# Attention and FFN in one kernel: the kernel plans the order of all engines itself

## The chip, the cores and the metric

The kernel runs on one core of one Trainium2 chip. The metric is the device time of one execution in microseconds (us), the median of 3 runs. Five instruction streams of the core matter here: TensorE (PE, with its weight loads PEld), VectorE (DVE), ScalarE (ACT), GpSimd (POOL), and SyncE (SP), which issues DMAs. Each stream runs its instructions in the order in which they were issued, so a waiting instruction holds up all that stand behind it on its engine.

## The reference, cut to what matters

Attention with 4 sink keys and a sliding window of 128 keys over 4 batches, 8 heads, 768 positions, head width 64; its output, heads side by side, is the 3072 x 512 input of an FFN with 2048 inner columns. All is float32.

```python
scores = scale * np.matmul(q, k.transpose(0, 1, 3, 2))
keep = is_sink | in_window            # in_window: 0 <= rel < window
scores = np.where(keep, scores, -1000000000.0)
scores = scores - np.max(scores, axis=-1, keepdims=True)
a = np.exp(scores)
a = a / (np.sum(a, axis=-1, keepdims=True) + 1e-09)
x = np.matmul(a, v)                   # then (B*S, H*D)
h = x @ w_in
g = np.where(pos, h, np.where(neg, 0.0, (h + beta) ** 2 / (4.0 * beta)))
return g @ w_out
```

The weights w_in and w_out arrive as 8-byte words (float64, read as pairs of int32), which the kernel turns into float32 by integer operations ("decoding").

## The kernel before

The 3072 rows are cut into 8 chunks of 384 rows (3 tiles of 128), first the first halves of the 4 batches, then the second halves. For each chunk attention is computed for 8 heads (a unit is one head of one chunk), its output is collected in `xn`, split into a high and a low part `x` (L617), and goes through the FFN.

- **FFN.** For each of 16 blocks j of 128 inner columns, `stage1` (L582) makes 12 matmuls of 384 columns into `h_ps` (high by high, high by low, low by high), then `g` by two ACTIVATEs on ACT (L595, L596) and one instruction on DVE (L597), then `gh` on ACT (L598) and `gl` by a subtraction (L599: on POOL for the first chunk, on DVE for the other seven). `stage2` (L602) makes 9 matmuls of 512 columns into three `o_ps`. It stands two j behind stage 1 (`LAG`), and the last two j of a chunk stand among the next chunk's first.
- **Attention.** The first 16 units (chunks 0 and 1) go through a path by pairs of heads in plain float32: `pair_scores` (L441 on PE, L452 on DVE, L457 on ACT), `early_transp` (L474, L476 on PE, copies on ACT), `pair_r` (L505), `pair_av` (L493, L496). The other 48 units ("native") split q, k, the probabilities and v into high and low parts, like the FFN (L254 to L405).
- **Decoding.** 16 blocks of 1 MB, by turns of w_in and w_out; each serves two j. A block takes four DVE instructions over 128 x 1024 elements (L170, L176, L179, L183) and one copy on ACT (L180). Nothing else than chunk 0's FFN waits for them, and all later chunks use the decoded weights again. Blocks 0 to 3 are loaded on SP's queue, the others on ACT's.
- **Order.** Chunk 0's attention (pairs 0 to 3, with blocks 0 to 3 decoded beside it and pair 4's scores) comes first, by a hand-written sequence (`first_pairs`, `queue`). Then the FFN of chunk c is mixed with the attention of chunk c+1 by `spread`: PE's order is that of the program, steps of both in proportion to their weights, and the decoding of blocks 4 to 15 is spread over chunk 0's FFN. On DVE, ACT, POOL and SP the framework's scheduler orders what is not tied down. The last chunk's FFN has no attention beside it.

Of the kernel before, what the change touches and what calls it, by code (L numbers as in the profile page):

```python
# [41 lines left out]
WLEAD = 0.9  # L42
# [7 lines left out]
def attn_ffn(ctx, tc, qk, qkp, vx, vs, par, w_in, w_out, out):  # L50
# [5 lines left out]
    moe3 = ctx.enter_context(tc.tile_pool(name="moe3", bufs=3))  # L56
    ps_a = ctx.enter_context(tc.tile_pool(name="ps_a", bufs=3, space=bass.MemoryType.PSUM))
# [98 lines left out]
    raw = {}  # L156
# [30 lines left out]
    def decode(t, w, words, pin=False):
        for f in decode_parts(t, w, words, pin):
            f()

    top = {}
    loaded = []

    def weights(n):

        def src(k):
            return (w_in, w_out)[k % 2][k // 2 * 2:k // 2 * 2 + 2].bitcast(I32).rearrange("j p c -> p j c")

        def fetch():
            for k in range(n, min(n + min(AHEAD if n > 2 else 1, NP // 2 - n // 2 - 1) + 1, NP)):  # L200
                if k not in raw:
                    raw[k] = wpool.tile([P, 2, 2 * DM], I32, name="w")

                    with tc.issue_after(loaded[-1]) if k < SYNC else nullcontext():
                        (nc.sync if k < SYNC else nc.scalar).dma_start(raw[k], src(k))

        def parts(on):
            j, i = n // 2 * 2, n % 2
            words = raw[n].rearrange("p j (c two) -> p j c two", two=2)
            if i:  # L210
                t = wpool.tile([P, 2, 2, DM], F32R, name="w")
                w_o[j:j + 2] = t[:, 0], t[:, 1]
            else:
                t = wi2[n // 2]
            return decode_parts(t, dec.tile([P, 2, DM], I32, name=f"bits{n % 2}"), words, pin=not on, on=on)

        def f():
            fetch()
            for g in parts(False):
                g()  # L220

        if n < WFIRST:
            return fetch, lambda: parts(True)
        return f


    again = {}
# [23 lines left out]
    fast.enter_context(tc.manual_schedule(engines={mybir.EngineType.PE}))  # L251
    st = {}

    def load(u):  # L254
        b, h, t0 = u
        T = CT * P
        W = (P if t0 else -NSINK) + CT * KB
        q_l = att.tile([P, T], F32R, name="q_l")
        q_h = att.tile([P, T], F32R, name="q_h")
        k_r = att1.tile([P, P + CT * KB], F32, name="k_r")[:, :W]  # L260
        k_s = att.tile([P, P + CT * KB], F32R, name="k_s")[:, :W]
        nc.sync.dma_start(k_r, qk[b, h, t0 // CT, :, T:T + W])
        q_r = att1.tile([P, T], F32, name="r")
        nc.sync.dma_start(q_r, qk[b, h, t0 // CT, :, :T])
        nc.scalar.copy(k_s, k_r)  # L265
        eng = nc.gpsimd if units.index(u) in KL_POOL else nc.vector
        eng.tensor_tensor(k_s[D:P], k_r[D:P], k_s[D:P].bitcast(F32), op=ALU.subtract)  # L267
        nc.scalar.copy(q_h, q_r)  # L268
        nc.gpsimd.tensor_tensor(q_l, q_r, q_h.bitcast(F32), op=ALU.subtract)  # L269
        st["qk", u] = ((q_h, q_l), k_s)  # L270

    def scores(u, i):
        b, h, t0 = u
        qs, k_s = st["qk", u]
        if i == 0:
            st["p", u] = [att.tile([P, CT, 260], F32, name="p"), att.tile([P, 2 * CT], F32, name="stat")]
# [4 lines left out]
        ps = ps_a.tile([P, 512], F32, name="ps_a")  # L281
        for j, q in enumerate(qs):
            nc.tensor.matmul(ps[:, lo:260], lhsT=q[:, i * P:(i + 1) * P], rhs=k_s[:, c0:c0 + 260 - lo],  # L283
                             start=(j == 0), stop=(j == len(qs) - 1))
        peak_i = peak[:, units.index(u), i:i + 1]
        m = (m0, m1, m2)[min(t, 2)]
        nc.vector.tensor_tensor_reduce(  # L287
            out=p[:, i, lo:260], in0=ps[:, lo:260], in1=m, scale=-0.125, scalar=3.0e38,
            op0=ALU.add, op1=ALU.min, accum_out=peak_i)
# [532 lines left out]
```

## Time and profile before

| what | value |
|---|---|
| time, median of 3 runs (lowest, highest) | 705.93 us (703.86, 706.32) |
| the profiled execution's own time | 705.98 us |
| its span, first to last instruction | 704.3 us |
| busy: PE, PEld | 681.5 us (97%), 604.6 us (86%) |
| busy: DVE, ACT, POOL | 510.3 us (72%), 489.5 us (70%), 278.8 us (40%) |
| DMA moved, mean rate | 73.98 MB, 105 GB/s |

Read it so: a busy PE is not a PE at its best rate, since an instruction that waits for data inside a run of matmuls, or runs at the lower clock, counts as busy as well. Two instructions of one engine overlap by some 0.05 to 0.1 us, so that a sum of durations is larger than the busy time of a stretch, which counts each moment once.

### The profile page before, as it was taken

How to read it: one execution, taken by the hardware profiler on the slowest of the kernel's cores; microseconds unless marked ns; L12 is line 12 of the kernel's file. 1: busy time of each engine (PE TensorE's matmuls, PEld its weight loads, DVE VectorE, ACT ScalarE, POOL GpSimd, SP SyncE). 2: the span in 40 equal slices, each digit the busy share in tenths (PEclk: the TensorE clock that was granted, in tenths of full speed). 3: DMA queues.
4: the chain of work that ended last, by engine and by line, in shares of the span. 5: the costliest groups of instructions: out<-in, count | busy, mean ns of one | idle time of the engine just before them, and what ended most of it. 6: DMA issues, size and time to landing. Idle time of an engine off the chain costs nothing.

```text
span 704.3 us, 12263 instructions
## 1 busy us (share of the span) xinstructions
PE 681.5 (97%) x3889; PEld 604.6 (86%) x3889; DVE 510.3 (72%) x1405; ACT 489.5 (70%) x1241; POOL 278.8 (40%) x470
## 2 busy tenths in 40 slices
PE   5899998999999999999999999999999999999996
PEld 3567877899999999989889999899899999989995
DVE  7888998887776877688777878878787877642221
ACT  4886667687778868777787877777776876554332
POOL 3003344744443445355554455635544444300000
PEclk9899999999999999999999999999999999999999
DMA  7864533132244344254333443434322310001001
GB/s 232 291 216 156 190 99 135 49 107 60 63 148 124 102 127 129 68 174 128 92 113 105 147 130 124 126 118 133 122 59 62 102 50 22 3 1 45 1 1 49
DMA packets 45441, 73.98 MB, mean 105 GB/s; under 512 B 10744, under 2 KB 30008, under 8 KB 45368
## 3 DMA queue, kind: packets, MB, share of 16 engines
q1 hardware_dynamic: 42104, 60.53, 28.2%
q10 hardware_dynamic: 3264, 12.58, 4.8%
q8 instruction: 33, 0.54, 0.3%
q14 instruction: 40, 0.33, 0.1%
HBM read 66.80 MB, written 6.29 MB: 104 GB/s over the span
## 4 chain that ended last, share of the span: by engine, by line
PE 79%; DVE 9%; DMA 3%; ACT 3%; POOL 3%; issue 2%; SPq 0%; ACTq 0%; POOLq 0%; DVEq 0%
PE h_ps L588 33%; PE o_ps L607 32%; PE ps_a L283 4%; PE ps_a L390 4%; PE ps_a L344 2%; DVE bits L176 2%; DVE bits L179 1%; DMA w<-w_in 1%; POOL q_l L269 1%; PE ps_a L474 1%; DVE w L183 1%; DVE bits L170 1%; PE ps_a L493 1%; DVE p L304 1%; DVE g L597 1%
## 5 line engine op out<-in xcount | busy, mean ns | idle before, releaser
L588 PE MATMUL h_ps<-x,wi 128*128 128x384 f32 x1536 | 310.2, 340 | 0.0
L588 PEld LDWEIGHTS h_ps<-x,wi 128*128 128x128 f32 x1536 | 262.2, 188 | 8.7 <-issue 1.5
L607 PE MATMUL o_ps<-w,gh 128*128 128x512 f32 x768 | 244.0, 398 | 0.0
L607 PE MATMUL o_ps<-w,gl 128*128 128x512 f32 x384 | 151.1, 393 | 0.4 <-POOL gl L599 0.4
L607 PEld LDWEIGHTS o_ps<-w,gh 128*128 128x128 f32 x768 | 134.3, 188 | 16.9 <-issue 1.7
L597 DVE SCALAR_TENSOR_TENSOR g<-g,h_ps 128x384 f32<-128x384 f32 x128 | 70.3, 549 | 61.7 <-ACT g L596 60.6
L595 ACT ACTIVATE g<-h_ps,half 128x384 f32<-128x384 f32 x128 | 73.9, 578 | 52.7 <-PE h_ps L588 52.0
L269 POOL TENSOR_TENSOR q_l<-r,q_h 128x384 fp32r<-128x384 f32 x48 | 51.1, 1064 | 122.7 <-ACT q_h L268 116.1
L598 ACT CAST gh<-g 128x384 fp32r<-128x384 f32 x128 | 65.5, 512 | 46.1 <-DVE g L597 44.9
L290 ACT ACTIVATE p<-p,peak 128x260 f32<-128x260 f32 (+1 forms) x144 | 71.5, 496 | 23.0 <-DVE peak L287 22.4
L607 PEld LDWEIGHTS o_ps<-w,gl 128*128 128x128 f32 x384 | 72.0, 188 | 17.8 <-POOL gl L599 0.7
L599 DVE TENSOR_TENSOR gl<-g,gh 128x384 fp32r<-128x384 f32 x112 | 67.3, 601 | 23.5 <-ACT gh L598 22.6
L267 DVE TENSOR_TENSOR k_s<-k_r,k_s 64x524 fp32r<-64x524 f32 (+1 forms) x44 | 49.1, 1115 | 34.4 <-ACT k_s L265 34.3
L596 ACT ACTIVATE g<-g 128x384 f32<-128x384 f32 x128 | 67.0, 524 | 2.0
L287 DVE CUSTOM_DVE_ANT_0 p<-ps_a,m 128x260 f32<-128x260 f32 (+1 forms) x144 | 57.0, 407 | 14.7 <-PE ps_a L283 13.8
L358 POOL TENSOR_SCALAR_AFFINE_SELECT pt<-pt 128x384 fp32r<-128x384 f32 (+1 forms) x96 | 51.3, 535 | 22.6 <-DVE pt L349 19.5
L304 DVE CUSTOM_DVE_ANT_0 p<-p,stat 128x128 f32<-128x128 f32 x128 | 57.0, 489 | 0.2
L356 POOL TENSOR_SCALAR_AFFINE_SELECT pt<-pt 128x384 fp32r<-128x384 f32 (+1 forms) x96 | 49.9, 521 | 8.8 <-ACT pt L348 4.9
L599 POOL TENSOR_TENSOR gl<-g,gh 128x384 fp32r<-128x384 f32 x16 | 23.4, 1461 | 67.7 <-ACT gh L598 64.2
L390 PEld LDWEIGHTS ps_a<-pt,v_s 128*128 128x128 f32 x304 | 42.4, 190 | 1.8
L390 PE MATMUL ps_a<-pt,v_s 128*128 128x256 f32 (+1 forms) x304 | 41.9, 275 | 0.0
L283 PE MATMUL ps_a<-k_s,q_h 128*128 128x260 f32 (+1 forms) x144 | 40.7, 283 | 1.2 <-DVE sk L352 0.9
(151 smaller groups left out, 933.1 us busy)
## 6 DMA issues: line engine op xcount, KB each, us to landing
r<-qk SPq DMA_DIRECT2D x48, 192.0 KB
k_r<-qk SPq DMA_DIRECT2D x32, 262.0 KB
again<-w_in SPq DMA_DIRECT2D x16, 512.0 KB
again<-w_out SPq DMA_DIRECT2D x16, 512.0 KB
w<-w_in ACTq DMA_DIRECT2D x6, 1024.0 KB
w<-w_out ACTq DMA_DIRECT2D x6, 1024.0 KB
out<-o SPq DMA_DIRECT2D x23, 256.0 KB
r<-vx SPq DMA_DIRECT2D x32, 128.0 KB
```

Source lines behind the costliest of these rows:

```text
L269: nc.gpsimd.tensor_tensor(q_l, q_r, q_h.bitcast(F32), op=ALU.subtract)
L283: nc.tensor.matmul(ps[:, lo:260], lhsT=q[:, i * P:(i + 1) * P], rhs=k_s[:, c0:c0 + 260 - lo], start=(j == 0), stop=(j == len(qs) - 1))
L290: nc.scalar.activation(p[:, i, lo:260], p[:, i, lo:260], AF.Exp, bias=peak_i, scale=-1.0, accum_out=stat[:, i:i + 1])
L304: nc.vector.tensor_tensor_reduce(out=own, in0=own, in1=p[:, i, 0:P], scale=r, scalar=0.0, op0=ALU.add, op1=ALU.add, accum_out=stat[:, i:i ...
L390: nc.tensor.matmul(z, lhsT=w, rhs=y, start=(n == 0), stop=(n == len(mms) - 1))
L588: nc.tensor.matmul(h_ps[:, :T], lhsT=w_i[j][:, w, ct * P:(ct + 1) * P], rhs=x[:, y, ct], start=(ct == 0 and n == 0), stop=(ct == NCT - 1 a ...
L595: nc.scalar.activation(g, h_ps[:, :T], AF.Relu, bias=half, scale=0.5)
L596: nc.scalar.activation(g, g, AF.Square)
L597: nc.vector.scalar_tensor_tensor(g, g, 1.0, h_ps[:, :T], op0=ALU.min, op1=ALU.max)
L598: nc.scalar.copy(gh, g)
L599: (nc.gpsimd if row0 == GL_POOL else nc.vector).tensor_tensor(gl, g, gh.bitcast(F32), op=ALU.subtract)
L607: nc.tensor.matmul(o_ps[tt], lhsT=gg[:, tt * P:(tt + 1) * P], rhs=w_o[j][:, w], start=(j == 0 and n == 0), stop=(j == NJ - 1 and n == 2))
```

## The change

The program no longer issues an instruction where the code stands. Each helper records an `op`: its engine, a length in ns, the call that issues it, and what it reads and writes (`Slot`s of a `Ring` stand for tiles that share buffers). `Plan.due` goes through PE's work in the order of the program and gives every op the latest time at which it is still of use; `Plan.order` then goes through all engines with those lengths, takes on each the ready op that is due first, and on PE the next one of two lanes, A (attention) and B (FFN), by their shares done. All instructions are then issued in that order, and no scheduler moves them on any engine.

With it come smaller edits. Decoding has other instructions: two that write single bytes into a tile `ends` (L361, L363), one that joins them with the shifted word in place (L365), the copy on ACT (L367), and the subtraction (L368): four on DVE, as before. All weight blocks are loaded on SP's queue. `gl` is computed on DVE for chunk 0 too. The values of a pair come by one DMA in place of four, and sink values from the tile `vq`, which needs no memset. Pair 4's scores are no longer in the first stage. For 2 of the native units a small addition moves from POOL to DVE (L459).

```diff
+    def due(self):
+        t = 0
+        for o in self.ops:
+            o.due = t + SOON
+            if o.eng == PE:
+                o.due = t
+                t += o.ns
+            for b in o.before:
+                b.after.append(o)
+        for o in reversed(self.ops):
+            for a in o.after:
+                o.due = min(o.due, a.due - o.ns - (2500 if o.eng == SP else DELAY[o.eng]))
...
+        def turn(t):
+            a, b = head("A"), head("B")
+            a_in, b_in = a is not None and not a.left and a.ready <= t, b is not None and not b.left and b.ready <= t
+            if a_in and b is not None and b_in:
+                if a.group[1] != b.group[1]:
+                    return a if a.group[1] < b.group[1] else b
+                ka, kb = ("A", a.group[1]), ("B", b.group[1])
+                return a if done[ka] * LEAD * total[kb] <= done[kb] * total[ka] else b
+            return a if a_in else b if b_in else None
...
-            first = nc.vector.tensor_scalar(w, x, 3, 0x3FFFFFFF, op0=ALU.logical_shift_left, op1=ALU.bitwise_and)
...
-            queue(nc.vector.scalar_tensor_tensor(w, x, -0x40000000, w, op0=ALU.bitwise_and, op1=ALU.bitwise_or), on)
...
-            queue(nc.vector.scalar_tensor_tensor(w, low, 29, w, op0=ALU.logical_shift_right, op1=ALU.bitwise_or), on)
-            queue(nc.scalar.copy(high, w.bitcast(F32)), on)
...
-            queue(nc.vector.tensor_tensor(rest, w.bitcast(F32), high.bitcast(F32), op=ALU.subtract), on)
...
+        op(SP, 420, lambda: nc.sync.dma_start(raw(), src()), r=[("w", past)] if past >= 0 else [], w=[r],
+           size=1 << 20)
+        op(DVE, 680, lambda: nc.vector.tensor_scalar(e()[..., 0], b()[..., 0, 3], 5, 0x07, op0=ALU.logical_shift_right,
+                                                     op1=ALU.bitwise_and), r=[r, "dec"], w=["ends"])
+        op(DVE, 680, lambda: nc.vector.tensor_scalar(e()[..., 3], b()[..., 1, 3], 0x80, 0xC0, op0=ALU.bitwise_and,
+                                                     op1=ALU.bitwise_xor), r=[r, "dec"], w=["ends"])
+        op(DVE, 1180, lambda: nc.vector.scalar_tensor_tensor(w(), words()[..., 1], 3, ends, op0=ALU.logical_shift_left,
+                                                             op1=ALU.bitwise_xor), r=["ends", "dec"], w=[wk, r])
+        op(ACT, 980, lambda: nc.scalar.copy(to()[:, :, 0], w().bitcast(F32)), r=[wk, "dec"], w=[(t, 0)])
+        op(DVE, 1180, lambda: nc.vector.tensor_tensor(to()[:, :, 1], w().bitcast(F32), to()[:, :, 0].bitcast(F32),
+                                                      op=ALU.subtract), r=[wk, (t, 0), "dec"], w=[(t, 1), t])
...
-        (nc.gpsimd if row0 == GL_POOL else nc.vector).tensor_tensor(gl, g, gh.bitcast(F32), op=ALU.subtract)
...
+        op(DVE, 500, lambda: nc.vector.tensor_tensor(gl(), g(), gh().bitcast(F32), op=ALU.subtract), r=[g, gh], w=[gl])
```

Three places show how the order moves. On PE, the end of chunk 0's attention and the first matmuls of its FFN (`h_ps<-x,wi`), before:

```order
L505 MATMUL ps_a<-ident,stat 64x128 x6
L493 MATMUL ps_a<-pt,vq_178 64x128 x2
L493 MATMUL ps_a<-pt,vq_178 64x256 x4
L493 MATMUL ps_a<-spn_179,vq_178 64x128
L493 MATMUL ps_a<-spn_180,vq_178 64x128
L441 MATMUL o_ps<-k_s,q_h 128x128 x2
L441 MATMUL o_ps<-k_s,q_h 128x260
L441 MATMUL h_ps<-k_s,q_h 128x260 x2
L441 MATMUL ps_a<-k_s,q_h 128x260
L474 MATMUL ps_a<-ident,p 128x128 x3
L588 MATMUL h_ps<-x,wi_155 128x384 x3
```

and now:

```order
L690 MATMUL ps_a<-ident,pt 128x128 x5
L692 MATMUL ps_a<-ident,pt 4x128
L690 MATMUL ps_a<-ident,pt 128x128 x5
L692 MATMUL ps_a<-ident,pt 4x128
L733 MATMUL ps_a<-ident,stat 64x128 x6
L811 MATMUL h_ps<-x,wi_155 128x384 x3
L713 MATMUL ps_a<-pt,vq_176 64x128 x2
L713 MATMUL ps_a<-pt,vq_176 64x256 x4
L713 MATMUL ps_a<-v_s,vq_176 64x128 x2
L648 MATMUL ps_a<-k_s,q_h 128x128 x2
L811 MATMUL h_ps<-x,wi_155 128x384 x3
```

The FFN's first matmuls move ahead of pair 3's product with the values and of all of pair 4, which stood in front of them. On DVE, the same place, before (`bits` is a block being decoded, `wi` a finished one, `xn` a pair's output):

```order
L183 TENSOR_TENSOR wi_156<-bits_389,wi_156 128x2x512
L464 TENSOR_SCALAR stat<-stat 128x2x3
L465 RECIPROCAL stat<-stat 128x2x3
L170 TENSOR_SCALAR bits_475<-w 128x1024
L496 TENSOR_TENSOR xn<-ps_a,xn 128x384
L176 SCALAR_TENSOR_TENSOR bits_475<-w,bits_475 128x1024
L619 TENSOR_TENSOR x<-xn,x 128x384
L179 SCALAR_TENSOR_TENSOR bits_475<-w,bits_475 128x1024
L496 TENSOR_TENSOR xn<-ps_a,xn 128x384
L452 ISA p,peak<-o_ps,m_109 128x128
```

and now:

```order
L363 TENSOR_SCALAR ends<-w 128x1024
L365 SCALAR_TENSOR_TENSOR w<-w,ends 128x1024
L361 TENSOR_SCALAR ends<-w 128x1024
L720 TENSOR_TENSOR xn<-ps_a,xn 128x384
L678 TENSOR_SCALAR stat<-stat 128x2x3
L680 RECIPROCAL stat<-stat 128x2x3
L368 TENSOR_TENSOR wi_155<-w,wi_155 128x2x512
L852 TENSOR_TENSOR x<-xn,x 128x384
L363 TENSOR_SCALAR ends<-w 128x1024
L365 SCALAR_TENSOR_TENSOR w<-w,ends 128x1024
L852 TENSOR_TENSOR x<-xn,x 128x384
```

Before, three blocks are finished here and the fourth is under way; now the first is just being finished and the second and third are three quarters done, and the fourth has not been begun. On POOL, chunk 0's FFN before (`gl` is the FFN's low part, `k_s` and `q_l` belong to native units):

```order
L599 TENSOR_TENSOR gl<-g,gh 128x384 x7
L267 TENSOR_TENSOR k_s<-k_r,k_s 64x392
L269 TENSOR_TENSOR q_l<-r,q_h 128x384
L599 TENSOR_TENSOR gl<-g,gh 128x384 x3
L267 TENSOR_TENSOR k_s<-k_r,k_s 64x392
L269 TENSOR_TENSOR q_l<-r,q_h 128x384
```

and on POOL now:

```order
L895 MEMSET ends 128x1024
L292 TENSOR_TENSOR tsel<-tsel_125 120x3
L426 TENSOR_TENSOR q_l<-r,q_h 128x384
L423 TENSOR_TENSOR k_s<-k_r,k_s 64x392
L426 TENSOR_TENSOR q_l<-r,q_h 128x384
L423 TENSOR_TENSOR k_s<-k_r,k_s 64x392
```

The 16 subtractions of `gl` are gone from POOL and stand among DVE's instructions. Up to the last instruction of decoding, DVE's queue holds the same 64 decoding instructions, 8 pairs and 15 `g` as before, 14 `gl` more, and the normalisation of one native unit instead of two.

## Rows read from the trace of the kernel before

**Rows 1.** The page, busy us of each engine, share of the span, instructions.
```profile
PE 681.5 (97%) x3889; PEld 604.6 (86%) x3889; DVE 510.3 (72%) x1405; ACT 489.5 (70%) x1241; POOL 278.8 (40%) x470
```
**Rows 2.** Windows of stages: length, busy (instructions) by engine, clock, DMA.
```profile
core 0: us, PE busy (x) PEld busy (x) DVE busy (x) ACT busy (x) POOL busy (x), PEclk, DMA share, GB/s
0.00:4.90 4.90, 0.05 (x2) 0.08 (x2) 3.56 (x19) 1.28 (x1) 1.37 (x11) 1.00 0.50 137
4.90:42.70 37.80, 30.16 (x223) 20.75 (x224) 31.62 (x101) 28.34 (x93) 5.13 (x25) 0.91 0.82 270
42.70:133.20 90.50, 88.34 (x531) 71.31 (x530) 80.79 (x140) 60.16 (x152) 37.72 (x30) 1.00 0.42 143
...
294.00:378.30 84.30, 83.71 (x474) 75.60 (x473) 65.28 (x192) 64.61 (x164) 43.25 (x72) 1.00 0.40 120
...
625.90:697.80 71.90, 71.82 (x360) 64.31 (x358) 21.08 (x41) 30.48 (x60) 0.00 (x0) 1.00 0.03 12
```
**Rows 3.** The chain that ended last: start, length, what.
```profile
4.95 7.92 DMA w<-w_in
...
359.68 3.23 DMA r<-vx
...
427.56 2.25 DMA r<-qk
...
687.40 2.08 PE o_ps L607 x9
689.48 2.08 PE h_ps L588 x12
```
**Rows 4.** Timeline of PE, first stage: start, length, what, idle before.
```profile
22.70 0.64 PE L441 MATMUL o_ps<-k_s,q_h 64*128 64x260 f32 x1
...
37.34 0.87 PE L505 MATMUL ps_a<-ident,stat 128*64 128x128 f32 x12
...
39.72 0.71 PE L441 MATMUL o_ps<-k_s,q_h 64*128 64x128 f32 x5
...
40.26 0.38 PE L441 MATMUL o_ps<-k_s,q_h 64*128 64x260 f32 x1
...
42.72 0.77 PE L588 MATMUL h_ps<-x,wi 128*128 128x384 f32 x3
```
**Rows 5.** Timeline of DVE, decoding and the next chunk's first split.
```profile
20.69 1.21 DVE L176 SCALAR_TENSOR_TENSOR bits<-w,bits 128x1024 int32<-128x1024 int32 x1
...
35.71 0.65 DVE L170 TENSOR_SCALAR bits<-w 128x1024 int32<-128x1024 int32 x1
...
89.09 1.93 DVE L179 SCALAR_TENSOR_TENSOR bits<-w,bits 128x1024 int32<-128x1024 int32 x1
...
131.99 1.23 DVE L183 TENSOR_TENSOR w<-bits,w 128x1024 fp32r<-128x1024 f32 x1 [0.65 <-ACT w L180]
133.53 2.31 DVE L619 TENSOR_TENSOR x<-xn,x 128x384 fp32r<-128x384 f32 x3 [0.32 <-ACT x L618]
```
**Rows 6.** Timeline of POOL beside the 1.93 us instruction.
```profile
88.54 1.39 POOL L599 TENSOR_TENSOR gl<-g,gh 128x384 fp32r<-128x384 f32 x1 [3.47 <-PE ps_a L474]
```
**Rows 7.** Groups: operation, shape, count, busy us, mean ns, idle before.
```profile
L599 DVE TENSOR_TENSOR gl<-g,gh 128x384 fp32r<-128x384 f32 x112 | 67.3, 601 | 23.5 <-ACT gh L598 22.6
...
L269 POOL TENSOR_TENSOR q_l<-r,q_h 128x384 fp32r<-128x384 f32 x48 | 51.1, 1064 | 122.7 <-ACT q_h L268 116.1
...
L179 DVE SCALAR_TENSOR_TENSOR bits<-w,bits 128x1024 int32<-128x1024 int32 x16 | 22.2, 1389 | 0.2
L176 DVE SCALAR_TENSOR_TENSOR bits<-w,bits 128x1024 int32<-128x1024 int32 x16 | 21.8, 1365 | 0.3
L170 DVE TENSOR_SCALAR bits<-w 128x1024 int32<-128x1024 int32 x16 | 11.4, 711 | 2.9 <-DMA w<-w_in 2.9
L183 DVE TENSOR_TENSOR wi<-bits,wi 128x1024 fp32r<-128x1024 f32 x8 | 10.6, 1326 | 4.4 <-ACT wi L180 4.4
L183 DVE TENSOR_TENSOR w<-bits,w 128x1024 fp32r<-128x1024 f32 x8 | 9.8, 1223 | 2.4 <-ACT w L180 2.4
```

More of the change, by code (lines that the diff above doesn't have):

```diff
@@ L1 @@
[L1 removed]
+import heapq
+from contextlib import ExitStack
 import concourse.bass as bass
@@ L187, in decode @@
[L187 to L210, printed above, removed]
+        nc.vector.tensor_scalar(w, x, 3, 0x3FFFFFFF, op0=ALU.logical_shift_left, op1=ALU.bitwise_and)
@@ L211, in parts @@
                 t = wpool.tile([P, 2, 2, DM], F32R, name="w")
                 w_o[j:j + 2] = t[:, 0], t[:, 1]
[L213 to L227, printed above, removed]
+                at["t"] = t
@@ L306, in scores @@
[L306 to L309 removed]
+        first = n < NATIVE + 2
+        op(DVE if first else POOL, 100 if first else 250, lambda: (nc.vector if first else nc.gpsimd).tensor_scalar(
+            stat()[:, CT:2 * CT], stat()[:, 0:CT], 1.0e-9, None, op0=ALU.add), r=[(stat, k) for k in range(CT)],
+           w=[(stat, "r")])
@@ L558, in attn_ffn @@
+        for f in steps:
+            f()
+        pair_load(n)
     chunks = [(b, t) for t in (0, CT) for b in range(B)]
@@ new lines, in mm, with at @@
+        def mm():
+            for n, (gg, w) in enumerate(((gh, 0), (gh, 1), (gl, 0))):
+                nc.tensor.matmul(ps(), lhsT=gg()[:, tt * P:(tt + 1) * P], rhs=w_o[j][:, w],
+                                 start=(j == 0 and n == 0), stop=(j == NJ - 1 and n == 2))
+        op(PE, 693, mm, r=[("w", j // 2 * 2 + 1), gh, gl], w=[ps])
+        if j == NJ - 1:
+            end = (row0, tt) == (last, CT - 1)
+            o = ("out",) if end else out_ring.new()
+            def at():
+                return xn.rearrange("p c t -> p (c t)")[:, :DM] if end else o()
+            op(ACT, 500, lambda: nc.scalar.copy(at(), ps()), r=[ps] + [("xn", c, a) for c in range(NCT) for a in range(2)]
+               if end else [ps], w=[o])
+            op(SP, 420, lambda: nc.sync.dma_start(out[row0 + tt * P:row0 + (tt + 1) * P, :], at()), r=[o], size=1 << 18)
@@ L624, in moe_steps @@
         o_ps, hs = [], {}
-        steps = [(0.0, lambda ct=ct: split(x, ct)) for ct in range(NCT)]
+        steps = [("B", 0.0, lambda ct=ct: split(x, ct)) for ct in range(NCT)]
         second = tail[:]
@@ L658, in attn_ffn, with run @@
-    pt0 = [att.tile([P, 2, CT, 2, P], F32R, name="pt").bitcast(F32).rearrange("p a i c q -> p (a i c q)")
-           for _ in range(2)]
-    wsteps = [weights(n) for n in range(NP)]
-    n0 = 0
+    ends = dec.tile([P, 2, DM], I32, name="ends")
+    spare = dec.tile([P, 2, 2 * DM], I32, name="spare")
+    with tc.issue_after(behind):
+        nc.gpsimd.memset(ends, 0)
+    p0 = [p_ring.new() for _ in range(2)]
+    pt0 = [pt_ring.new() for _ in range(2)]
+    def run(steps, c):
+        for lane, w, f in steps:
+            plan.group = lane, c, w
+            f()
@@ L697, in attn_ffn @@
-    other = const.tile([1, 1], I32, name="other")
-    nc.vector.tensor_scalar(flag[0:1, 2:3], flag[0:1, 1:2], -1.0, 1.0, op0=ALU.mult, op1=ALU.add)
-    nc.vector.tensor_copy(other, flag[0:1, 2:3])
-    for _, f in prev + tail:
-        f()
+        b, t0 = chunks[c]
+        ffn = moe_steps(b * S + t0 * P, tail)
+        n1 = min(H * (c + 2), len(units)) + 2
+        attn = [step for n in range(n0, n1) for step in attn_steps(n)] if n0 < n1 else []
+        n0 = n1
+        if c == 0:
+            attn = [step for m in range(4, 9) for step in pair_steps(m)] + attn
+            ffn = spread([("B", 1.0, lambda n=n: block(n)) for n in range(4, NP)], ffn, LEAD)
@@ new lines, in result @@
+    def result():
+        nc.vector.tensor_reduce(flag[0:1, 1:2], ps()[0:1, :P], axis=mybir.AxisListType.X, op=ALU.min)
+        nc.vector.tensor_scalar(flag[0:1, 2:3], flag[0:1, 1:2], -1.0, 1.0, op0=ALU.mult, op1=ALU.add)
+        nc.vector.tensor_copy(other, flag[0:1, 2:3])
+    op(DVE, 4000, checks, w=["flag", "both"] + [("peak", n, i) for n in range(len(units)) for i in range(CT)])
+    ps = bank_a.new()
+    op(PE, 110, lambda: nc.tensor.transpose(ps()[0:1, :P], flag[:, 0:1], ident), r=["flag"], w=[ps])
@@ L703, in attn_ffn @@
+    op(DVE, 700, result, r=[ps], w=["flag"])
+    plan.issue()
+    region.close()
     fast.close()
```

778 lines of the change are left out of this document (472 added, 306 removed).

## The prediction

> **What bounds the kernel now.** I read the page's busy times first: PE is busy 97% of the span, DVE 72%, ACT 70%, POOL 40% [rows 1]. So PE bounds the kernel, and a new order can gain only where PE waits or runs below its best rate. Next, what PE's best rate is: at the end of the chain of waits, where the last chunk's FFN stands alone, 12 matmuls of stage 1 take 2.08 us (the chain groups them by turns with stage 2's 9, which take 2.08 us too) [rows 3]. A step j of the FFN is then 4.16 us, a chunk 16 x 4.16 = 66.6 us, and the 8 chunks 533 us.
>
> The windows then say where PE falls short [rows 2]. The last chunk alone: 71.9 us, which is 17.3 steps of 4.16 (its own 16 and the rest of the chunk before): at its best rate. A middle chunk takes 84.3 us with 83.7 of them busy, 17.7 us over the FFN's 66.6 us, in which the 8 native units' matmuls stand: nothing in this row looks like waiting. The first 133.2 us are another matter. The FFN's first matmul starts at 42.72 us [rows 4], and chunk 1 gets its first low part of x at 133.5 us [rows 5]. The work of PE to that point is 62.4 us of FFN (16 steps without the 4.16 us of the last two steps' stage 2, which come later), 8 pairs, and some 4 us of the first native units (an estimate: a middle chunk's 17.7 us are 2.2 us a unit, for less than two). A pair at full clock takes 5 us: from pair 3's L505 at 37.34 to the next pair's scores at 39.72 are 2.4 us, its transposes and scores about as much [rows 4]. That is 62.4 + 40 + 4 = 106 us against 133.2, so some 27 us are lost there: 4.9 before the first matmul, a few to the lower clock (the first stage's clock is 0.91 on the mean, and a matmul of 260 columns shows 0.64 us at 22.7 us, where 0.38 us stands at 40.3 us [rows 2, 4]), and the rest to waiting.
>
> What does PE wait for there? For DVE. DVE is busy 3.56 + 31.62 + 80.79 = 116.0 of these 133.2 us, 87%, more than anywhere later (77% in the middle chunk) [rows 2]. The 16 blocks of decoding are 11.4 + 21.8 + 22.2 + 10.6 + 9.8 = 75.8 us of it by durations [rows 7], and the last ends at 133.2 us, just before chunk 1's split [rows 5]. PE shows 88.34 of 90.5 us busy in the middle window of it [rows 2], since its instructions overlap; the sum above is the better measure.
>
> **The change, part by part.** The question is when DVE can finish decoding, and whether PE, ACT or DMA takes its place.
>
> *Decoding, on DVE.* Four instructions go, four come, so overlap cancels. The quiet prices are 0.65 us for the one-source instruction (L170) and 1.21 to 1.23 us for those with two sources [rows 5]. Their means are higher, 0.71 and 1.22 to 1.39 us [rows 7], because some take up to 1.93 us while POOL works at a subtraction [rows 5, 6]. The new block is two one-source instructions and two with two sources. Single bytes in and out do not occur on DVE in this trace, so their price is bounded: 0.65 us (the one-source row of as many elements) to 1.22 us (the two-source row) each, and above that only if bytes are handled worse than words. I take 0.65 us, the row of the same operation. With it a block is 2 x 0.65 + 2 x 1.22 = 3.74 us, 16 are 60 us; I add 2 us for the POOL work that remains: 75.8 - 62 = 14 us saved (between 16 saved and, at 1.22 us a byte instruction, 4 lost).
> [...]
>
> *gl on DVE.* 14 of the 16 stand before the last block: 14 x (0.60 - 0.08 of overlap) = 7.3 us added [rows 7]. It also takes away the 1.39 us subtractions on POOL that slow DVE [rows 6], which is in the sum above.
>
> *The rest of DVE's queue to that point.* One native unit's normalisation stands behind it now: -1.2 us; the two memsets of the value tiles are gone: -1 us; both are estimates from DVE's mean of 0.45 us an instruction (116.0 us for 260). Sum: 116.0 - 14 + 7.3 - 2.2 = 107 us of work (105 to 125 by the bounds of the byte instructions).
>
> *DVE's idle time* to that point is 133.2 - 116.0 = 17.2 us: 1.3, 6.2 and 9.7 us in the three windows [rows 2]. The first two stay by my reckoning. ACT carries 28.3 us in the 37.8 us of the first stage, and loses there about one cast and one pair's six exponentials, some 4 us of the 28: with 24 us of work after the first scores, ACT holds the FFN's start to no earlier than 30 us, ten us before now, and DVE waits for it in between. The third window is what an order by due time can fill: I halve it. DVE then ends decoding at 107 + 1.3 + 6.2 + 5 = 119.5 us (112 if nearly all idle time goes, 124 if all stays).
>
> *PE to the same point* needs its 106 us, 4.9 us of start and some 3 us at the lower clock: 114 us at the least, so PE does not forbid 119.5 us but leaves little below it.
>
> *Loads.* Block 0's load goes behind pair 2's two on SP's queue; those wait for buffers that pair 0's scores free. Now it is issued at 4.95 us and takes 7.92 us to land [rows 3], with DMA at 270 GB/s in that stage [rows 2]: bandwidth sets most of that, so I count 0 to 3 us later, covered by pair 1's and 2's scores, which DVE now has ahead of the first decoding; without that cover it costs 3 us. The twelve blocks that leave ACT's queue for SP's are paced by decoding and cost nothing while DMA stands at 42% [rows 2].
>
> *Later chunks.* PE's order of A and B steps there is almost the same as before, and PE runs there without visible waits, so I count 0 (between 4 us won and what the second rival costs). The end of the last chunk is unchanged.
>
> **Sum.** Chunk 1 starts at 119.5 instead of 133 us: -13.5 us. The profiled execution has 705.98 us with a span of 704.3, and stands at the median of 705.93: 705.98 - 13.5 = 692.5, I say 692 us.
>
> **The rivals.**
> 1. *The gain stays small*: DVE keeps all its idle time because PE, DVE and ACT hand over in turn (matmul, two ACTIVATEs, L597, cast, gl) and gl now queues behind instructions of 1.2 us each. The 9.7 us idle in the FFN's window speak for it; that gl no longer waits for 1.39 us of POOL against it. DVE ends at 124 to 130 us: 696 to 703 us, 700 in the middle.
> 2. *SP's one queue and the one buffer `r` become the bound of the later chunks.* `r` holds by turns a unit's q and its v: 2.25 us of load, 1.06 us of POOL's q_l, 3.23 us of load [rows 3, 7], and two casts on ACT and one subtraction on POOL that cost at most as much as q_l each: 6.5 to 9.7 of the 10.5 us a unit has (84.3 / 8). All engines now run in one planned order, and a load that stands behind an output DMA or a weight check on SP holds up PE, which has its next unit's scores in a fixed place. Against it: the same buffer and queue serve now, without a wait in the middle chunk's row. It decides at 13.5 / 48 = 0.3 us a native unit; with 0.5 us it is +24 - 13.5 = +10.5: 716 us, slower.
> 3. *Bytes cost DVE as much as two sources do, or more*: at 1.22 us, 32 x 0.57 = 18 us more: DVE ends at 137.5 us, 4.5 us behind now: 710 us, slower. It turns slower from 0.65 + 13.5 / 32 = 1.07 us an instruction.
> 4. *Writing every other word is slow*: L365 at the slowest two-source row, 1.93 us [rows 5], in 15 blocks: 15 x 0.71 = 10.7 us, DVE ends at 130 us: 703 us. [...]
> 5. *The plan does more than that*: PE's floor of 114 us is reached and the later chunks win up to 4 us: 682 to 687 us.
>
> **How the numbers follow.** The forecast (687 to 697 us about 692) has 0.55, rival 1 0.12, rival 2 0.07, rival 3 0.06, rival 4 0.06, rival 5 0.12, and 0.02 is left for a gain and a loss that cancel. What a measurement of this kernel can tell from no change is about 0.5%, 3.5 us: 702.4 to 709.5 us. Faster than that: the forecast, rival 5, nearly all of rival 1 and half of rival 4, 0.81. The same: the edge of rival 1, half of rivals 3 and 4 and what cancels, 0.08. Slower: rival 2, half of rival 3 and the rest, 0.11. The range that holds 8 in 10 goes from rival 5's 682 to 709 us, where rival 3 begins; the forecast's own is 687 to 697.
>
> **What would show each step.** The first FFN matmul at 30 to 35 us instead of 42.7. The byte instructions at 0.65 to 0.75 us, L365 and L368 at 1.2, none near 2 us. The last decoding's end at 115 to 124 us and chunk 1's first split there too; from then on middle chunks of 84.3 us as now, and the last at 71.9. I am wrong if the byte instructions show over 1 us, if the middle chunks are longer than 85 us with PE waiting for loads of `r`, or if the last decoding ends early and chunk 1 still starts at 130 us.

## The result, and the profile after

| | before | after |
|---|---|---|
| time, median (lowest to highest), 4 runs each on the same chip | 705.59 us (703.86 to 706.32) | 693.20 us (692.49 to 694.62) |
| ratio after / before, 95% interval | | 0.9831 (0.9806 to 0.9855) |
| profiled execution, its span | 705.98 us, 704.3 us | 692.49 us, 690.4 us |

The kernel is faster by 12.4 us, 1.7%. The busy times of the whole span hardly show it (compare [rows 1]); PE has the same 3889 matmuls:

```profile
PE 674.4 (98%) x3889; PEld 603.1 (87%) x3889; DVE 509.6 (74%) x1421; ACT 487.2 (71%) x1241; POOL 240.5 (35%) x421
```

The windows of the kernel after, cut at its own stages (start, attention before the FFN, chunk 0's FFN up to the last decoding, a middle chunk, the last chunk; columns as in [rows 2]):

```profile
0.00:4.60 4.60, 0.00 (x0) 0.01 (x1) 2.23 (x14) 1.28 (x1) 1.38 (x11) 1.00 0.47 127
4.60:28.40 23.80, 21.72 (x192) 16.07 (x192) 20.11 (x80) 20.31 (x76) 4.86 (x23) 1.00 0.82 264
28.40:119.80 91.40, 89.73 (x552) 71.79 (x551) 85.43 (x170) 66.70 (x163) 9.74 (x8) 1.00 0.52 181
282.20:365.40 83.20, 83.20 (x476) 76.54 (x475) 66.69 (x192) 63.95 (x164) 39.12 (x64) 1.00 0.41 122
610.90:683.30 72.40, 72.24 (x362) 64.78 (x360) 21.01 (x39) 31.21 (x61) 0.00 (x0) 1.00 0.03 12
```

Against [rows 2]: the first stage is 23.8 us instead of 37.8, with PE busy 91% of it instead of 80% and at a printed clock of 1.00 instead of 0.91 (the last section says where that column is not to be trusted). The stage of chunk 0's FFN is as long as it was (91.4 and 90.5 us), with more of pair 3 and all of pair 4 in it. A middle chunk is 1.1 us shorter than the 84.3 us of before, the last one is the same within 0.5 us. DVE works 2.23 + 20.11 + 85.43 = 107.8 us to the end of decoding, 116.0 before.

PE's timeline where the FFN begins (start, length, instructions), and DVE's where decoding ends and chunk 1 begins (L852 is the split of `xn` into `x`), to set against [rows 4, 5]:

```profile
27.61 0.87 PE L733 MATMUL ps_a<-ident,stat 128*64 128x128 f32 x12
28.41 0.80 PE L811 MATMUL h_ps<-x,wi 128*128 128x384 f32 x3
```

```profile
118.56 1.22 DVE L368 TENSOR_TENSOR w<-ends,w 128x1024 fp32r<-128x1024 f32 x1
...
121.42 1.42 DVE L852 TENSOR_TENSOR x<-xn,x 128x384 fp32r<-128x384 f32 x2
```

The FFN's first matmul is at 28.41 us (42.72 before), the last decoding ends at 119.8 us (133.2), and chunk 1's first split is at 121.4 us (133.5).

**Where PE's time went.** The same 3889 matmuls run in both, so the difference can be summed on PE itself: for each matmul, the time until the next one starts, less the interval that its shape keeps in a steady run (0.173 us for 384 columns, 2.08 / 12 of [rows 3]). What is left over is lost, to waits and to the lower clock above all; it is shown by stretches of the trace:

| PE's lost time, us | 0 to 40 us | 40 to 140 us | later | sum |
|---|---|---|---|---|
| before | 18.6 | 13.8 | 12.1 | 44.5 |
| after | 11.6 | 9.4 | 9.0 | 30.0 |

So 7.0 us of the 14.5 were won in the first 40 us, 4.4 in chunk 0's FFN (1 us of it at a native unit's transposes, which waited for DVE for 1.9 us before, L344, and wait for 0.9 us now, L525), and 3.1 in the later chunks. How large a loss comes out hangs on the intervals taken, the differences hardly: with 0.45 ns a column (0.173 us / 384) for every shape they are 6.9, 4.3 and 3.2 us. The span shrinks by 13.9 us, since the tail behind the last matmul is 0.6 us longer. The list of PE's waits, of both kernels over the whole span (instruction <- what it waited for: us in all, times, longest), shows how the first stage won:

```profile
PE o_ps L441 <- DMA q_h<-qkp: 4.8, 1, 4.8
PE ps_a L474 <- DVE peak L452: 2.9, 2, 2.4
PE ps_a L474 <- ACT xn L507: 2.5, 3, 1.1
PE ps_a L344 <- DVE p L302: 1.9, 1, 1.9
PE ps_a L474 <- ACT p L457: 1.6, 4, 1.0
...
```

```profile
PE o_ps L648 <- DMA q_h<-qkp: 4.6, 1, 4.6
PE ps_a L690 <- DVE stat L678: 1.6, 1, 1.6
PE ps_a L525 <- DVE p L469: 0.9, 1, 0.9
...
PE ps_a L690 <- ACT pt L699: 0.5, 1, 0.5
...
```

Before (the first list), the early transposes (L474) waited 7.0 us, in the lines shown, for DVE's masked maxima (`peak`) and ACT's exponentials and copies. In the second list they (L690) wait 2.1 us. Where the longest of these waits ended before, an instruction of decoding (L179) stands between the maxima on DVE:

```profile
15.88 1.22 DVE L179 SCALAR_TENSOR_TENSOR bits<-w,bits 128x1024 int32<-128x1024 int32 x1
...
17.36 0.42 DVE L452 CUSTOM_DVE_ANT_0 pt<-ps_a,m 128x260 f32<-128x260 f32 x1
...
17.94 0.52 PE L474 MATMUL ps_a<-ident,pt 128*128 128x128 f32 x3 [2.38 <-DVE peak L452]
```

No wait for a decoded weight is in either list; the experiments come back to that.

### The profile page after: what moved, and what is told of

Read it like the earlier page. It is cut to its first block, busy times and chain, and to the rows that moved or that the text cites. A ratio compares the mean times of both kernels' runs of the same rounds, so it can differ in the third digit from the quotient of the medians.

```text
span 690.4 us, 11991 instructions
## 1 busy us (share of the span) xinstructions
PE 674.4 (98%) x3889; PEld 603.1 (87%) x3889; DVE 509.6 (74%) x1421; ACT 487.2 (71%) x1241; POOL 240.5 (35%) x421
## 4 chain that ended last, share of the span: by engine, by line
PE 90%; DVE 5%; ACT 2%; DMA 1%; issue 1%; SPq 0%; POOL 0%; DVEq 0%; ACTq 0%
PE h_ps L811 37%; PE o_ps L834 37%; PE ps_a L587 5%; PE ps_a L444 5%; PE ps_a L525 2%; DMA w<-w_in 1%; PE ps_a L713 1%; PE ps_a L690 1%; PE ps_a L648 1%; DVE x L852 1%; PE ps_a L733 1%; PE ps_a L602 1%; DVE p L471 0%; DMA q_h<-qkp 0%; DVE gl L823 0%
## 5 line engine op out<-in xcount | busy, mean ns | idle before, releaser
L823 DVE TENSOR_TENSOR gl<-g,gh 128x384 fp32r<-128x384 f32 x128 | 78.9, 616 | 31.1 <-ACT gh L822 30.1
L452 ACT ACTIVATE p<-p,peak 128x260 f32<-128x260 f32 (+1 forms) x144 | 71.7, 498 | 40.9 <-DVE peak L449 40.3
L471 DVE CUSTOM_DVE_ANT_0 p<-p,stat 128x128 f32<-128x128 f32 x128 | 62.4, 512 | 2.4
L498 POOL TENSOR_TENSOR v_s<-r,v_s 128x256 fp32r<-128x256 f32 (+1 forms) x48 | 37.2, 774 | 37.4 <-ACT v_s L497 31.7
L444 PE MATMUL ps_a<-k_s,q_l 128*128 128x260 f32 (+1 forms) x144 | 40.4, 281 | 0.0
```

The lines of the kernel that those rows point to most:

```text
L444: nc.tensor.matmul(ps()[:, lo:260], lhsT=q()[:, i * P:(i + 1) * P], rhs=k_s()[:, c0:c0 + 260 - lo], start=(j == 0), stop=(j == len(qs) - 1))
L452: op(ACT, 400 if lo else 500, lambda: nc.scalar.activation(p()[:, i, lo:260], p()[:, i, lo:260], AF.Exp, bias=peak[:, n, i:i + 1], scale=-1.0,
L471: nc.vector.tensor_tensor_reduce(out=own, in0=own, in1=p()[:, k, 0:P], scale=r, scalar=0.0, op0=ALU.add, op1=ALU.add, accum_out=stat()[:, ...
L823: op(DVE, 500, lambda: nc.vector.tensor_tensor(gl(), g(), gh().bitcast(F32), op=ALU.subtract), r=[g, gh], w=[gl])
```

## The experiments

Each kernel is timed beside the kernel before on the same chip. "After" below is the changed kernel with its 693.2 us; FFN start, last decoding and split are read from the profiles as above.

**1. The new order with the old decoding.**

```diff
-        op(DVE, 680, lambda: nc.vector.tensor_scalar(e()[..., 0], b()[..., 0, 3], 5, 0x07, op0=ALU.logical_shift_right,
...
-        op(DVE, 680, lambda: nc.vector.tensor_scalar(e()[..., 3], b()[..., 1, 3], 0x80, 0xC0, op0=ALU.bitwise_and,
...
-        op(DVE, 1180, lambda: nc.vector.scalar_tensor_tensor(w(), words()[..., 1], 3, ends, op0=ALU.logical_shift_left,
...
+        op(DVE, 620, lambda: nc.vector.tensor_scalar(ends, words()[..., 1], 3, 0x3FFFFFFF, op0=ALU.logical_shift_left,
...
+        op(DVE, 1180, lambda: nc.vector.scalar_tensor_tensor(ends, words()[..., 1], -0x40000000, ends,
...
+        op(DVE, 1180, lambda: nc.vector.scalar_tensor_tensor(w(), words()[..., 0], 29, ends, op0=ALU.logical_shift_right,
...
```

> The changed kernel with the four old decoding instructions on DVE (one with one source, three with two), planned and issued in its way. A block costs DVE 0.65 + 3 x 1.22 = 4.31 us by the quiet rows of before, where the byte form costs 0.77 + 0.77 + 1.23 + 1.22 = 3.99 us: 16 x 0.32 = 5 us more work. Theory A (DVE's queue sets when chunk 1 starts): decoding ends 5 us later, at 125 us, and the time rises by 4 to 6 us, to 697 to 699 us. Theory B (the order alone makes the gain; DVE has slack beside PE's floor of 114 us): under 1.5 us more, 693 to 695 us.

Measured: 696.66 us (694.28 to 697.51), ratio 0.9861 (0.9841 to 0.9880). FFN start 30.4, last decoding 124.9, split 125.3 us. It fell between the two ranges, nearer to theory A's, whose 125 us for the end of decoding it meets. Against after it is 3.5 us slower by the medians and 2 us by the ratios, whose intervals overlap. The new order and the smaller edits that came with it, without the new decoding, make 9.5 of the 12 us.

**2. The new instructions in the kernel before**, ordered as before: the byte decoding, and `gl` of chunk 0 on DVE.

```diff
-GL_POOL = 0
+GL_POOL = None
...
+            first = nc.vector.tensor_scalar(be[..., 0], bw[..., 0, 3], 5, 0x07, op0=ALU.logical_shift_right,
+                                            op1=ALU.bitwise_and)
...
+            queue(nc.vector.scalar_tensor_tensor(value, x, 3, w, op0=ALU.logical_shift_left, op1=ALU.bitwise_xor), on)
```

> The kernel before, still ordered by its scheduler, with the byte form of decoding and with gl of chunk 0 on DVE. By theory A DVE's work to the last decoding falls by 10 us (decoding, its slowing by POOL included) and rises by 7 (gl): 113 us; its idle time stays at 17 us, so that chunk 1 starts 3 us earlier: 702 to 704 us, and the other 9 us of the gain belong to the order. If the instructions make most of the gain (theory C): 694 to 698 us. If the scheduler's order fits the new instructions worse: 706 us or more.

Measured: 705.08 us (704.07 to 706.87), ratio 0.9985 (0.9973 to 0.9998). DVE's work to the last decoding fell to 109.7 us and that end came at 127.5 us, 5.7 us earlier than before; the first split came at 131.6 us, only 1.9 earlier, as much as the FFN's start (40.9 against 42.7 us). The time lies 1 us above theory A's range. A DVE that is done sooner was worth 1 us.

**3. One more byte instruction a block** (the first of the two issued twice: 16 x 0.77 = 12.3 us more on DVE).

```diff
+        op(DVE, 680, lambda: nc.vector.tensor_scalar(e()[..., 0], b()[..., 0, 3], 5, 0x07, op0=ALU.logical_shift_right,
+                                                     op1=ALU.bitwise_and), r=[r, "dec"], w=["ends"])
```

> The changed kernel with the first byte instruction of each block issued twice: 16 x 0.65 to 0.77 us = 10 to 12 us more on DVE's queue before the last decoding and nothing else. Theory A: 8 to 12 us later, 701 to 705 us. Theory B (slack on DVE): under 4 us, below 697 us.

Measured: 703.14 us (702.09 to 704.25), ratio 0.9955 (0.9939 to 0.9971): 10 us given back. The FFN still begins at 27.9 us, but PE's list of waits from 80 to 132 us now has what neither list above had:

```profile
PE h_ps L813 <- DVE wi L370: 1.6, 1, 1.6
PE o_ps L836 <- ACT w L369: 1.4, 1, 1.4
PE h_ps L813 <- ACT wi L369: 1.0, 1, 1.0
PE o_ps L836 <- DVE w L370: 1.0, 1, 1.0
```

PE waits 5 us for decoded weights (`wi`, `w`; L813 and L836 are the FFN's matmuls). So the changed kernel stands just beside this bound: 12 us more on DVE are felt nearly in full.

**4. Chunk 0's gl back on POOL.**

```diff
-        op(DVE, 500, lambda: nc.vector.tensor_tensor(gl(), g(), gh().bitcast(F32), op=ALU.subtract), r=[g, gh], w=[gl])
+        pool = row0 == 0
+        op(POOL if pool else DVE, 1200 if pool else 500, lambda: (nc.gpsimd if pool else nc.vector).tensor_tensor(
+            gl(), g(), gh().bitcast(F32), op=ALU.subtract), r=[g, gh], w=[gl])
```

> The changed kernel with chunk 0's gl on POOL again. Theory A with POOL's disturbance: DVE loses 7 us of work and its decoding instructions are stretched again by about 6 us, so the time stays within 2 us, 691 to 696 us, and two-source instructions near 2 us stand beside POOL's subtractions. If POOL's subtractions did not slow DVE: 5 to 7 us faster, 686 to 688 us. If gl's longer way over POOL held up PE: 696 to 700 us.

Measured: 690.77 us (689.97 to 692.97), ratio 0.9786 (0.9765 to 0.9806), 2.4 us better than after by the medians, though the two ratios' intervals touch. The expectation had a gap where it fell. The last decoding ends at 115.1 us, 4.7 earlier, and the split comes only 0.9 us earlier; DVE's timeline shows both, with other work between:

```profile
113.84 1.22 DVE L368 TENSOR_TENSOR w<-ends,w 128x1024 fp32r<-128x1024 f32 x1
...
120.47 1.48 DVE L854 TENSOR_TENSOR x<-xn,x 128x384 fp32r<-128x384 f32 x3
```

The end of decoding does not set the start of chunk 1 there. POOL's cost to DVE shows in the same trace, POOL first, then DVE beside it:

```profile
69.14 1.14 POOL L824 TENSOR_TENSOR gl<-g,gh 128x384 fp32r<-128x384 f32 x1 [2.76 <-ACT gh L822]
```

```profile
68.19 1.21 DVE L368 TENSOR_TENSOR w<-w 128x1024 fp32r<-128x1024 f32 x1
69.33 2.03 DVE L368 TENSOR_TENSOR wi<-w,wi 128x1024 fp32r<-128x1024 f32 x1
```

The same instruction takes 1.21 us just ahead of POOL's subtraction (but for its last 0.26 us) and 2.03 us beside it.

**5. Program order on DVE, ACT and POOL** in place of the due times.

```diff
-                    heapq.heappush(ready[e], (o.due, o.n, o))
+                    heapq.heappush(ready[e], (o.n if e in (DVE, ACT, POOL) else o.due, o.n, o))
```

> The changed kernel, but on DVE, ACT and POOL the planner takes the ready op that stands first in the program and not the one that is due first; PE's lanes and SP stay as they are. If the due times make the gain (DVE does decoding that PE waits for later than attention that PE waits for now), the FFN's first matmul moves from 28.4 back by 3 us or more and DVE is idle longer than 12 us before the last decoding: 696 to 702 us. If the gain comes from PE's two lanes and from all engines being planned together, and program order is good enough for the others, it stays within 2 us of the changed kernel: 691 to 695 us.

Measured: 703.57 us (700.58 to 704.75), ratio 0.9968 (0.9954 to 0.9982): 10 of the 12 us are gone, a little more than expected. FFN start 36.0 us, split 129.6 us, but the last decoding ends at 112.2 us, earlier than in any other kernel here. The trace is of the fastest of the 12 executions, 700.58 us, and so shows 8 of the 10 us; where the rest goes is not shown. PE's waits in the first 45 us, and DVE's timeline at the longest of them:

```profile
PE ps_a L690 <- DVE peak L658: 4.9, 3, 2.9
PE o_ps L648 <- DMA q_h<-qkp: 4.3, 1, 4.3
...
```

```profile
24.46 1.22 DVE L368 TENSOR_TENSOR w<-w 128x1024 fp32r<-128x1024 f32 x1
...
26.72 0.29 DVE L658 CUSTOM_DVE_ANT_0 pt<-o_ps,m 128x128 f32<-128x128 f32 x1
```

In the changed kernel the same maxima (pair 3's) come 8 us earlier, and most of that decoding stands behind them:

```profile
18.90 0.28 DVE L658 CUSTOM_DVE_ANT_0 pt<-o_ps,m 128x128 f32<-128x128 f32 x1
...
20.55 0.29 DVE L658 CUSTOM_DVE_ANT_0 pt<-o_ps,m 128x128 f32<-128x128 f32 x1
20.76 0.08 DVE L658 DVE_READ_ACCUMULATOR2_ANT peak<- 128x1 f32 x1
20.76 0.76 DVE L361 TENSOR_SCALAR ends<-w 128x1024 uint8<-128x1024 uint8 x1
```

Ahead of the last of pair 3's maxima DVE has done 11 decoding instructions in the kernel before, 13 in this one and 5 in the changed kernel. The wait seems to cost twice: in this kernel PE's granted clock is lower as well, as it was before: 1.00 from 10 to 20 us, then a mean of 0.83 in each of the next two windows. In windows of 1 us the kernel before prints 0.50 from 20 to 23 and from 31 to 33 us, and 1.00 from 24 to 30 and from 34 to 40 us. Windows of this kernel, then of the kernel before, then of the changed one:

```profile
10.00:20.00 10.00, 6.06 (x55) 3.99 (x55) 6.84 (x25) 7.80 (x29) 1.29 (x3) 1.00 0.99 356
20.00:30.00 10.00, 6.24 (x48) 4.47 (x49) 9.93 (x24) 7.21 (x21) 0.00 (x0) 0.83 0.60 183
30.00:40.00 10.00, 9.70 (x85) 7.24 (x84) 8.59 (x14) 7.66 (x22) 0.00 (x0) 0.83 0.96 361
```

```profile
20.00:30.00 10.00, 8.07 (x62) 5.42 (x62) 8.93 (x23) 8.31 (x28) 0.91 (x2) 0.83 0.71 219
30.00:40.00 10.00, 9.45 (x84) 6.87 (x84) 9.23 (x24) 7.86 (x26) 0.00 (x0) 0.83 0.89 307
```

```profile
10.00:20.00 10.00, 8.42 (x92) 6.29 (x92) 7.54 (x33) 8.83 (x36) 1.21 (x3) 1.00 0.96 338
20.00:30.00 10.00, 9.52 (x91) 6.58 (x89) 8.90 (x20) 10.00 (x34) 0.00 (x0) 1.00 0.76 252
30.00:40.00 10.00, 9.40 (x61) 7.06 (x56) 9.95 (x28) 8.83 (x25) 0.00 (x0) 1.00 0.60 213
```

By PE's ledger this kernel loses 18.7 us in the first 40, as much as before, but only 8.9 us in the later chunks, as little as after.

**6. PE in program order**, the other engines with their due times.

```diff
-                    times = [o.ready for o in (head("A"), head("B")) if o is not None and not o.left]
+                    nxt = min((o for o in (head("A"), head("B")) if o is not None), key=lambda o: o.n, default=None)
+                    times = [nxt.ready] if nxt is not None and not nxt.left else []
```

> The changed kernel, but PE takes its instructions in the order of the program (the steps spread by their weights, as before the change) and not the next ready one of two lanes; the other engines keep their due times. If PE's lanes make the gain, since they let the FFN begin before pair 3's product, the FFN's first matmul goes back to 32 us or later and the whole to 697 to 704 us. If the order on DVE, ACT and POOL makes it, this kernel stays within 3 us of the changed one: 691 to 696 us, with the last decoding at 118 to 123 us.

Measured: 693.92 us (693.05 to 694.44), ratio 0.9832 (0.9811 to 0.9854): the same as after. The FFN starts at 30.1 us. PE's two lanes make nothing that can be measured; the order on the other engines does it.

**7. and 8. Program order on DVE alone, and on ACT alone.** The edit is that of experiment 5 with `e == DVE`, then with `e == ACT`.

> The changed kernel with program order on DVE alone; ACT and POOL keep their due times. With program order on DVE, ACT and POOL the FFN began at 36.0 us and PE waited there 4.9 us for DVE's masked maxima (L658), which stood behind decoding. If DVE's queue alone makes that, this kernel gives the same: FFN's start at 35 to 36 us, 701 to 704 us. If ACT's casts of the decoding make a good part of it, the start is at 30 to 33 us: 696 to 699 us.

> The changed kernel with program order on ACT alone; DVE and POOL keep their due times. If DVE's order makes the whole gain, this one stays within 2 us of the changed kernel: FFN's start at 28 to 30 us, 692 to 695 us. If casts of the decoding that stand ahead of exponentials on ACT matter too, the start is at 30 us or later: 695 to 699 us.

Measured: DVE alone 705.55 us (704.55 to 707.40), ratio 0.9998 (0.9983 to 1.0013); ACT alone 700.35 us (699.83 to 701.15), ratio 0.9925 (0.9908 to 0.9943). Both are slower than expected, and in both expectations I had bound the time to the FFN's first matmul, which is a bad measure: it stands at 30.7 and 26.6 us here, while pair 3 and 4 are left behind and the split comes at 128.6 and 124.5 us. With DVE alone, one wait in the first 45 us is enough:

```profile
PE ps_a L690 <- DVE peak L658: 6.3, 2, 6.0
```

A second loss, in the later chunks, shows in these two traces, where one engine is out of step with the others: PE's waits in one middle chunk, with DVE in program order and then with ACT (none in the changed kernel, nor such a loss in the one trace of experiment 5):

```profile
PE ps_a L444 <- DVE xn L593: 1.4, 2, 0.8
```

```profile
PE ps_a L444 <- DVE xn L606: 1.1, 2, 0.7
...
```

Three of the middle chunks take 83.8 to 85.3 us there, as against 82.0 to 83.2.

**9. Two native units moved from chunk 0's stage to chunk 1's**, and **10. the same with gl on POOL.**

```diff
-            attn = [step for m in range(4, 9) for step in pair_steps(m)] + attn
+            attn, n0 = [step for m in range(4, 9) for step in pair_steps(m)], NATIVE
```

> The changed kernel, but the first two native units (PE, DVE, ACT and POOL work of some 2.2 us of PE each) move from the stage of chunk 0's FFN to that of chunk 1's. If DVE's work up to the last decoding sets the end, some 2 to 3 us of it leave, PE's floor of that stage falls by 4 us too, and PE fills the later stage with the units as well as it does now: the two stages together take as long on PE, so what is gained is the idle time of the first, 1 to 4 us: 689 to 692 us. If chunk 1's stage has no room (its PE is busy 79.9 of 80.2 us), the 4 us come back there and nothing is gained: 692 to 695 us; the first split of chunk 2 tells: earlier than 201.6 us or not.

> Chunk 0's gl on POOL and the two native units in chunk 1's stage. With gl on POOL the last decoding ended at 115.1 us but chunk 1 began at 120.5 us, so DVE no longer set the start there and PE's own work did. If that is so, taking 4 us of PE's work out of the stage lets the start follow the decoding, and the two add up: 686 to 689 us. If the work is only moved, the result is the one with gl on POOL alone, 689 to 692 us.

Measured: 698.18 us (696.19 to 700.15), ratio 0.9894 (0.9872 to 0.9915), and 695.90 us (695.51 to 698.71), ratio 0.9871 (0.9846 to 0.9896): both slower than after, the second with an interval that just overlaps after's but clearly slower than experiment 4, and both outside both ranges of my expectations. Chunk 1 starts 3.7 us earlier (117.7 us) and takes 4.4 us more (84.6 against 80.2 us), so the work is only moved; beyond that PE now waits for the units' own preparation, and the next chunk is 1.9 us longer. PE's waits from 117 to 285 us in experiment 9; the changed kernel has 0.2 us there:

```profile
PE ps_a L444 <- POOL q_l L426: 1.5, 2, 0.7
...
```

By this reading the two units done ahead are the lead that keeps PE from waiting later; the waits in the list add up to some 2 of the 5 us lost, so that this is argued and not shown.

**11. gl on POOL for every other j of chunk 0** (as experiment 4, with `row0 == 0 and j % 2 == 0`).

> Chunk 0's gl on POOL for every other j and on DVE for the rest. With all 16 on POOL it was 690.8 us, with all on DVE 693.2 us. If PE's own work sets the start of chunk 1 in both, it is between them or equal to the better: 690 to 693 us. If POOL's subtraction stretches the DVE instructions beside it as much as it saves, it is nearer to 693 us; the last decoding's end should lie between 115.1 and 119.8 us either way.

Measured: 692.95 us (692.71 to 693.83), ratio 0.9826 (0.9806 to 0.9845): no gain over after, and the last decoding at 121.0 us lies outside what I expected. The fastest version is that of experiment 4; why half of its change is worth nothing was not followed further.

## Why the prediction came out right, point by point

The time, 692 us against 693.2, and the terms of the sum were close:

| step | predicted | measured |
|---|---|---|
| decoding on DVE, by durations | -14 us | -9.8 us |
| gl on DVE | +7.3 us | +7.0 us |
| rest of DVE's queue (what remains) | -2.2 us | -5.4 us |
| DVE's work to the last decoding | 107 us | 107.8 us |
| DVE idle to there | 12.5 us | 12.0 us |
| last decoding's end | 119.5 us | 119.8 us |
| FFN's first matmul | 30 to 35 us | 28.4 us |
| chunk 1's first split | 119.5 us | 121.4 us |
| chunks 1 to 6 | 0 | -2.9 us |
| last chunk and its tail | 0 | +1.1 us |

That the time came out so near is in part luck. The miss on the bytes was made up by the rest of DVE's queue. Chunk 1 starts 12.1 us earlier and not 13.5, and the later chunks, which the sum counted as nothing, make up for that.

- *Byte instructions.* They take 0.765 us by their median, not 0.65, as this table by groups (to 121 us; count, then busy us and mean ns) shows; 32 x 0.115 = 3.7 us is most of the miss of the term. Rival 3 (1.22 us) is out: it needed 1.07.

```profile
L365 DVE SCALAR_TENSOR_TENSOR w<-w,ends 128x1024 int32<-128x1024 int32 x14 | 17.2, 1226 | 0.4
L363 DVE TENSOR_SCALAR ends<-w 128x1024 uint8<-128x1024 uint8 x14 | 11.0, 787 | 0.0
L361 DVE TENSOR_SCALAR ends<-w 128x1024 uint8<-128x1024 uint8 x14 | 10.7, 767 | 2.2 <-DMA w<-w_in 2.1
L368 DVE TENSOR_TENSOR wi<-w,wi 128x1024 fp32r<-128x1024 f32 x8 | 10.6, 1319 | 0.4 <-ACT wi L367 0.4
L823 DVE TENSOR_TENSOR gl<-g,gh 128x384 fp32r<-128x384 f32 x15 | 8.5, 568 | 0.4 <-ACT gh L822 0.4
```

- *Hopping writes.* L365 writes every other word in 15 of the 16 blocks and takes 1.226 us by its median in 14 of them; the other, of 1.89 us, stands beside work on POOL. In the last block it writes adjacent words and takes 1.226 us too, so rival 4 is out. Hopping reads cost no more either: L176 reads every other word and takes 1.21 us, L183 on adjacent ones 1.23 us [rows 5].
- *The rest of DVE's queue.* The native units' work before the last decoding fell by 3.4 us, not 1.2, perhaps since POOL stretches less of it; these 2.2 us more cover over half of the miss on the bytes. It is an attribution from the traces, not tried by itself.
- *Rivals 1, 2 and 5.* DVE did not keep its idle time (12.0 of 17.2 us). SP's one queue cost nothing: middle chunks are shorter, with no wait for loads. Of rival 5 the later chunks' gain did come, 2.9 us, but PE did not reach its floor of 114 us: chunk 1 starts at 121.4.

**The step that was wrong** is the link "the end of decoding sets the start of chunk 1". The number followed from it, but the runs cut the two apart. Decoding ends 7.6 us earlier in experiment 5 and the kernel is 10 us slower; in 4 it ends 4.7 us earlier for 0.9 us at the split; in 2 it ends 5.7 us earlier than before for 1.9. By these runs, what set the start before was PE's own work plus what it lost in the first 40 us, when its transposes waited for maxima and exponentials, some of which stood behind decoding, and its granted clock fell to a mean of 0.83 from 20 to 40 us. The due times put the decoding behind (5 of its instructions ahead of pair 3's last maximum, not 11 as before or 13 as in experiment 5), and without the due times 10 of the 12 us are lost (5). The smaller edits of the change are in experiment 5 as well, so that they, the planning and the new decoding make 2 us without the due times; apart from `gl` none of the small ones was run by itself. The cheaper decoding pays, as far as it does, because the work put off must still be in time: with the old instructions the gain falls by 2 to 3.5 us (1), with 12 us more on DVE by 10 (3). The two ends agreed in the changed kernel because it stands close to both limits.

I had the pieces in the profile: the waits of the first stage and the clock of 0.91. I put them down as "a few us" of PE's loss and followed DVE's total.

What stays open: the 2.4 us of experiment 4, and how the 7.0 us of the first 40 divide exactly between waiting and clock. The listed waits give an estimate: they fall from 7.0 to 2.1 us, which is 4.9, and leave some 2 us for the lower clock.

## What to carry to other kernels

An engine with a long queue of work that is needed later should do first what another engine needs now: order by due time was worth 10 us here with the same instructions, and cheaper instructions without it 1 us. Order all engines by the same rule: with DVE alone in program order 12 us were lost and with ACT alone 7, as against 10 with both and POOL in it. Sum the bounding engine's own lost time by stretches before trusting the end of another engine's work as the bound: two ends that coincide are not cause and effect until an experiment moves one of them.

## What the runs showed of the hardware that was not expected

- A one-source DVE instruction on 128 x 1024 single bytes, read eight bytes apart and written four apart, takes 0.765 us by its median (L361, L363) where the same count of 4-byte words takes 0.65 us [rows 5]: not equal to it, and far below the two-source 1.22 us.
- The granted clock of PE was 1.00 in each window of the changed kernel from 10 to 40 us, with PE busy 8.4 to 9.5 us of 10; with program order on DVE, ACT and POOL it was 0.83 from 20 to 30 and from 30 to 40 us, and PE had been busy 6.1 and 6.2 us of the 10 before each.
- The clock column prints 1.00 for the first 10 us of the kernel before and of the changed one, but the matmuls say otherwise: one of 260 columns takes 0.64 us there, as at 22.7 us of the kernel before, where the column prints 0.50, and not the 0.38 us of 40.3 us [rows 4], where it prints 1.00. In the kernel before 0.64 us still stands at 12.58 us (first line), in the changed one (the other two) at 8.04 us, and 0.38 us at 9.17 us. So by these durations PE runs at first at the rate that it has at a printed 0.50, until some 13 us before and some 9 us after. By them the 0.91 of [rows 2] is too high by this stretch, and so is the 1.00 of the changed kernel's first stage.

```profile
12.58 0.64 PE L441 MATMUL ps_a<-k_s,q_h 64*128 64x260 f32 x1
```

```profile
8.04 0.64 PE L648 MATMUL o_ps<-k_s,q_h 64*128 64x260 f32 x1
...
9.17 0.38 PE L648 MATMUL ps_a<-k_s,q_h 64*128 64x260 f32 x1
```
